# Sink scores of an attention and token-mixer kernel: from full-array matmuls to four array tiles of 64 rows by 32 columns

## The chip, the cores and the metric

The kernel runs on one core of a Trainium2 chip. A core has a matrix engine (TensorE, PE in the profile, its weight loads PEld), VectorE (DVE), ScalarE (ACT), GpSimd (POOL) and SyncE (SP), which take their instructions from five queues in order, and DMA engines. Operands lie in SBUF, matmul results in PSUM, both with 128 partitions. The metric is the time of one execution on the device in microseconds.

## The reference

Attention with a sliding window and a few sinks, followed by a mixer block, in one launch:

```python
batch, n_heads, seq, head_dim = (4, 8, 768, 64)
n_sink, window = (4, 128)
scores = scale * np.matmul(q, k.transpose(0, 1, 3, 2))
keep = is_sink | in_window          # key < 4, or 0 <= query - key < 128
a = softmax(np.where(keep, scores, -1e9))
x = a @ v                           # heads side by side: (4, 768, 512)
h = np.maximum(x.T @ w_tok1, 0) @ w_tok2      # over tokens, 768 -> 256 -> 768
u = x + h.T
out = u + np.maximum(u @ w_ch1, 0) @ w_ch2    # over channels, 512 -> 1536 -> 512
```

A query needs its own block of 128 keys, the block before, and the first four keys (the sinks). For queries of the first two blocks the sinks lie in those blocks; for the other four blocks, 512 queries a head, the scores of the four sinks are a product of their own. That product is what the change is about.

## The kernel before, in words

The 32 heads are handled as 16 pairs (`pairs`, four to a batch), the 768 tokens as six tiles of 128. q and k of a pair are turned so that the 64 elements of a head's vectors lie on partitions, head 0 of the pair on 0 to 63, head 1 on 64 to 127 (tiles qT2 and kT). The stages of a pair:

- `transposed` (line 452; `turn`, line 432, for the first five pairs) turns q and k through TensorE, with one matmul on rows 0 to 63 of the array and one on rows 64 to 127 in turn, into two PSUM banks. `prepare` lists the copies out of PSUM, among them `sink_columns`, which copies the four sink columns of each head into `kTs`.
- `scores(p, g)` (line 486): the window scores of key blocks 2g and 2g+1, again with matmuls on half of the rows, one head each, `ps[:, i]` being another bank for each head i. Exp on ScalarE (line 509), a mask on VectorE or, early on, added by TensorE (`masked`).
- `score_sinks(p)` (line 530): the sink scores of pairs p-1 and p, two matmuls over all 128 rows and 128 columns that add up in one bank (`ps_sk`), then one Exp on ScalarE into `pT_sink` (line 542). It runs once for two pairs, eight times in all.
- `sink_values` and `values` (or `pv` in the first batch and for the last pair): the weighted sums, which begin with the sinks' part; a reciprocal and a product on VectorE write `x_sb` (line 615).

`kTs` holds, for each place of a pair in its batch, a block of 128 partitions by two heads by 64 columns. It is zero but for the sinks' keys: head i's rows, in its own 64 columns, at column 0 for an even pair and at column 32 (`ODD`) for an odd one. So in the full-array product, partition 64i + c of the result holds head i of the even pair for c = 0 to 3 and of the odd pair for c = 32 to 35; the other partitions are zero, and the zero rows of `v_sink` drop them later.

`mix_h`, `mix_u` and `turned_u` do the token mixing and turn its result (`uT`, two copies out of two banks); `mix_channels(b)` has the channel mixing of a batch: 12 `v1` tiles by two halves of the tokens (four matmuls of 384 columns each, copied out with a relu), then 72 output matmuls of 512 columns in groups of three.

The kernel divides PSUM into two slots of two banks with the tag sc and four single banks with the tag mx. Everything that is not scores or transposed pairs takes mx.

The order of all instructions is decided by a planner while the program is built. A `unit` is a run of TensorE work with a cost, its dependencies, the banks it needs (all free at its start) and the work on other engines that follows. A `burst` joins several `piece`s that use half the rows into one unit, with the banks of all. `Plan.run` goes through three lists: `first` (the first batch's attention, `first_attention`, line 782), `main` (the channel mixing) and `side` (attention and token mixing of the other batches, `attention_and_tokens`, line 806), each in its own order. Between main and side it takes whichever can begin sooner, with a target for how far side should be. A change between units that use half the rows and all others is charged `SWITCH` (line 214). Costs and times of the planner only decide the order; on the chip the engines wait for each other through semaphores.

On the side, a pair p has two bursts: the first with the next pair's transposes, scores of g = 0 and the sink values of the pair before; the second with the scores of g = 1 and 2 and, for two of the four pairs of a batch, `turned_u`. For an even hp the unit `score_sinks(p + 1)` stands just before that second burst. All matmuls go through the helper `mm` (line 109), so their rows in the profile carry its line.

Of the kernel before, what the change touches and what calls it, by code (L numbers as in the profile page):

```python
# [16 lines left out]
def kernel(  # L17
# [14 lines left out]
    B, H, S, D = q.shape  # L32
    P = 128
# [7 lines left out]
    NHP = H // 2  # L41
# [21 lines left out]
    def bank(tag, *shape, dtype=FP32, slot=None):  # L63

        n = given[tag].pop(0) if slot is None else slot
        return psum.tile([P, *shape], dtype, name=f"ps_{tag}", tag=f"{tag}{n}", bufs=1)
# [41 lines left out]
    def mm(*args, **kwargs):  # L108
        in_order(nc.tensor.matmul(*args, skip_group_check=True, **kwargs))  # L109
# [19 lines left out]
    done = {}  # L129
    tiles = {}  # L130
# [7 lines left out]
    def keep_warm(n, slot):  # L138
# [18 lines left out]
        out=ident, in_=ident, compare_op=ALU.not_equal, fill=1.0, base=0, pattern=[[-1, P]], channel_multiplier=1,  # L157
    ))
    in_order(nc.gpsimd.affine_select(
        out=mask_add[:, :, 0], in_=mask_add[:, :, 0], compare_op=ALU.is_ge,  # L160
# [3 lines left out]
        out=mask_add[:, :, 1], in_=mask_add[:, :, 1], compare_op=ALU.is_ge,  # L164
# [10 lines left out]
    kTs = [kTs0[:, n] for n in range(NHP)]  # L175
# [5 lines left out]
    ODD = D // 2  # L181
# [3 lines left out]
    for n in range(4):  # L185
        i, odd = n // 2, n % 2
        rows = slice(D * i + ODD * odd, D * i + ODD * odd + n_sink)
        in_order(nc.sync.dma_start(  # L188
            out=v_sink_f[rows, odd::2, i, 0:D],
# [167 lines left out]
    def unit(ns, fn, deps=(), need=None, then=(), half=False):  # L357

        op = Op({"PE": float(ns)}, fn, deps, then, size=float(ns))
        for f in then:  # L360
            if op not in f.deps:
                f.deps.append(op)
        op.need = need or {}
        op.half = half
        return op

    def burst(*pieces):

        need = {}
        for p in pieces:  # L370
            for tag, banks in p.need.items():
                need.setdefault(tag, []).extend(banks)

        def run():
            for p in pieces:
                p.fn()

        op = unit(
            sum(p.size for p in pieces), run, [d for p in pieces for d in p.deps], need,
            [t for p in pieces for t in p.then], half=True,  # L380
        )
        for p in pieces:
            for key in p.keys:
                done[key] = op
        return op

    def piece(ns, fn, deps, need, then, keys=()):
        op = Op({}, fn, deps, then, size=float(ns))
        op.need, op.keys = need, keys
        return op  # L390
# [41 lines left out]
    def turn(p, n):  # L432

        name = ("q", "k")[n]

        def run():
            ps = [bank("mx", NT, D, dtype=BF16) for _ in range(2)]
            tiles["ps_" + name, p] = [t.rearrange("d j p -> d p j") for t in ps]
            for j in range(NT):
                for x in range(2):  # L440
                    rows = ds(D * x, D)
                    in_order(nc.tensor.transpose(ps[x][:, j], bfs[p, n][rows, j], ident[rows, rows]))

        readers = [[op] for op in done[name + "T", p]]
        if n:
            readers[0].append(done["kTs", p])
        done["t" + name, p] = unit(
            180, run, [done[name + "_bf", p]], {"mx": readers}, [op for r in readers for op in r], half=True,
        )
        return done["t" + name, p]  # L450
# [20 lines left out]
    def masked(p, g):  # L471

        def run():
            ps = tiles["ps_s", p, g] = bank("sc", 2, 4 * P)
            for i in range(2):
                mm(
                    ps[:, i, 0:width(g)], ident,
                    mask_adds[g == 0].rearrange("p k n q -> p (k n q)")[:, 0:width(g)], start=True, stop=False,
                )

        x = done["exp", p, g] = Op({}, None)
        deps = [done["tk", 0]] if p == 0 else []
        done["mask", p, g] = unit(width(g) * 0.84, run, deps, {"sc": [[x]]})
        return done["mask", p, g]
# [43 lines left out]
        return piece(width(g) * 0.47, run, deps, {} if by_pe else {"sc": [[x]]}, then, [("s", p)])  # L528

    def score_sinks(p):  # L530
        def run():
            pT_sink = pt_pool.tile([P, (NT - 2) * P], BF16, name="pT_sink")
            tiles["ps_sk", p] = bank("mx", (NT - 2) * P)
            for n in (p - 1, p):
                tiles["pT_sink", n] = pT_sink
                mm(
                    tiles["ps_sk", p], kTs[n % NHP].rearrange("p i c -> p (i c)"), tiles["qT", n][:, 2 * P:],
                    start=(n < p), stop=(n == p),
                )

        def exp(e):
            in_order(nc.scalar.activation(tiles["pT_sink", p], tiles["ps_sk", p], AF.Exp, scale=scale))

        x = Op({"ACT": 580.0}, exp, [done["pv", p - 2]] if p >= 2 else [])
        u = unit(432, run, [d for m in (p - 1, p) for d in [done["kTs", m], *done["qT", m]]], {"mx": [[x]]}, [x])
        for n in (p - 1, p):
            done["p", n, NT] = x
            done["sk", n] = u
        return u

    def pv(p, half):
        b, hp = pairs[p]
# [229 lines left out]
    def first_attention():  # L782

        for p in range(NHP):
            prepare(p)
        turned = [turn(p, n) for p in range(NHP) for n in range(2)]
        masks, scored, out = [], [], []
        for p in range(NHP):
            for g in range(NT // 2):
                if (p, g) in MASKED_BY_PE:  # L790
                    masks.append(masked(p, g))
                scored.append(burst(scores(p, g)))
                if g == 0 and p == NHP - 1:
                    scored.append(score_sinks(p))
            if p == 1:
                out.append(score_sinks(p))
            if p % 2:
                out += [pv(n, half) for n in (p - 1, p) for half in range(2)]
        tokens = []
        for g in range(2):  # L800
            tokens.append([mix_h(0, g, t, 1) for t in range(NTOK)])
            tokens[g] += [mix_u(0, g, st, 2, g == 0 or st == 2) for st in range(0, NT, 2)]
            tokens[g] += [transpose_u(0, g, st, 2) for st in range(0, NT, 2)]
        return scored, masks, turned, out, *tokens[::-1]

    def attention_and_tokens():

        parts, units = [], []
        first, last = NHP, len(pairs) - 1
        prepare(first)  # L810
        units += [turn(first, n) for n in range(2)]
        for p in range(first, last + 1):
            b, hp = pairs[p]
            pieces = []
            if p < last:
                prepare(p + 1)
                pieces.append(transposed(p + 1))
            pieces.append(scores(p, 0))
            if p > first:
                pieces.append(sink_values(p - 1))  # L820
            if p == last:
                pieces.append(turned_u(b, 0, "sc"))
            units.append(burst(*pieces))
            if p > first:
                units += [values(p - 1, i) for i in range(2)]
            pieces = [scores(p, 1), scores(p, 2)]
            if hp == 0 and p > first:
                units.append(mix_h(b - 1, 1, 0, NTOK))
                units += [mix_u(b - 1, 1, st, 2) for st in range(0, NT, 2)]
                pieces.append(turned_u(b - 1, 1))  # L830
            if hp == NHP - 1 and p < last:
                pieces.append(turned_u(b, 0))
            if hp % 2 == 0:
                units.append(score_sinks(p + 1))
            units.append(burst(*pieces))
            units[-1].then.append(sink_rows(p))
            if hp == 2:
                units.append(mix_h(b, 0, 0, NTOK))
                units += [mix_u(b, 0, st, 2) for st in range(0, NT, 2)]
            if hp == 0 and p > first:  # L840
                parts.append(units)
                units = []
        units += [pv(p, half) for half in range(2)]
        units.append(mix_h(b, 1, 0, NTOK))
        units += [mix_u(b, 1, st, 2) for st in range(0, NT, 2)]
        units.append(burst(turned_u(b, 1)))
        return parts + [units]
# [162 lines left out]
    plan.pending.append(done["masks"])  # L1010

    first = first_attention()
    main, side, sizes = [], [], []
    parts = attention_and_tokens()
    for b in range(B):
        units = parts[b] if b + 1 < B else []
# [53 lines left out]
```

## Time and profile before

| what | value |
|---|---|
| time, median of 3 runs (lowest to highest) | 209.58 us (209.21 to 210.65) |
| the profiled execution, its own time | 209.46 us |
| its span, first to last instruction | 207.7 us |
| mean granted TensorE clock | 0.998 |
| busy in 0 to 20 us: PE, VectorE, ScalarE, GpSimd | 15.94, 13.46, 15.54, 14.86 us |
| busy in 55 to 80 us: the same | 24.63, 17.37, 12.01, 22.10 us |
| busy in 120 to 150 us: the same | 29.61, 18.32, 17.93, 0.00 us |
| Exp of the sinks, x8, mean | 0.60 us |
| uT copy of 128x768 on VectorE / on ScalarE | 0.56 / 0.82 us |

A row of the timeline gives the start and the length of a run of equal instructions, both in us, the engine, the line in the kernel, the operation, what is written and read, `rows*columns` of the array for a matmul, the shape, and how many; in brackets the idle time of the engine ahead of it and what ended it. Lengths of matmuls overlap, since the next one enters the array while the last is still on its way through; distances between starts tell what the stream costs. A few matmul records are missing from the trace, weight loads are all there. The chain of waits is the path that ended last, followed back from the last instruction.

### The profile page before, as it was taken

The numbers are of one execution on the slowest core, as the hardware profiler recorded it, in microseconds if no ns is written. First come the engines' busy times: TensorE is split into PE (matmuls) and PEld (weight loads), VectorE is DVE, ScalarE is ACT, GpSimd is POOL, SyncE is SP. The second block draws the span as 40 slices with busy tenths as digits, with TensorE's granted clock in tenths as the row PEclk, the third lists the DMA queues.
The fourth block names the chain that finished last, engine by engine and source line by source line (L and its number), as shares of the span: only waits on it lengthen the run. The fifth ranks groups of instructions, "written<-read, shape, count | busy, mean of one in ns | idle before, by whom it ended". The sixth has DMA issues, their size and how long they took to land.

```text
span 207.7 us, 5034 instructions
## 1 busy us (share of the span) xinstructions
PE 198.0 (95%) x2126; PEld 119.3 (57%) x2145; DVE 114.3 (55%) x252; ACT 114.4 (55%) x202; POOL 67.5 (32%) x86
## 2 busy tenths in 40 slices
PE   6699999999999999999999999999999999999994
PEld 2345975566665665557656645666666445665443
DVE  4786664777577675867576552767674421000222
ACT  4799668878727435867684241868751103774000
POOL 6399759794699980720000000000000000000000
PEclk9999999999999999999999999999999999999999
DMA  6999999999999999795000212100001122000222
GB/s 198 283 260 182 172 174 191 156 164 201 156 159 176 185 206 195 52 70 37 3 0 5 101 51 104 51 5 0 3 0 49 56 101 101 3 0 0 101 104 101
DMA packets 73222, 21.57 MB, mean 104 GB/s; under 512 B 63216, under 2 KB 70256, under 8 KB 73200
## 3 DMA queue, kind: packets, MB, share of 16 engines
q0 software_dynamic: 67232, 11.80, 71.9%
q1 hardware_dynamic: 5968, 9.45, 12.9%
q8 instruction: 17, 0.28, 0.6%
q14 instruction: 5, 0.04, 0.1%
HBM read 26.75 MB, written 6.29 MB: 159 GB/s over the span
## 4 chain that ended last, share of the span: by engine, by line
PE 83%; DMA 6%; DVE 4%; ACT 2%; issue 2%; POOL 1%; SPq 0%; POOLq 0%; DVEq 0%
PE ps_mx L109 75%; PE ps_sc L109 5%; DMA w_tok<-in_moe_w_tok_dram 4%; DMA v_sink_f<-in_v_dram 2%; PE ps_sc L460 2%; DVE x_sb L615 1%; ACT qT L116 1%; DVE kT L118 1%; POOL v_aug L102 1%; PE ps_mx L745 1%; ACT v1T L122 1%; DVE recip L612 1%; PE ps_mx L112 1%; POOL v_sink L118 0%; SPq L188 0%
## 5 line engine op out<-in xcount | busy, mean ns | idle before, releaser
L109 PE MATMUL ps_mx<-uT,w_ch 128*128 128x384 bf16 x384 | 68.3, 326 | 0.9 <-DVE x_sb L615 0.9
L109 PE MATMUL ps_mx<-w_ch,v1T 128*128 128x512 bf16 (+2 forms) x299 | 64.2, 362 | 0.9 <-issue 0.3
L122 ACT ACTIVATE v1T<-ps_mx 128x384 bf16<-128x384 f32 x74 | 36.3, 493 | 33.7 <-PE ps_mx L109 22.9
L109 PEld LDWEIGHTS <-w_ch 128*128 128x128 bf16 x384 | 35.5, 98 | 25.0 <-DVE x_sb L615 2.5
L109 PEld LDWEIGHTS <-v1T 128*128 128x128 bf16 x312 | 28.9, 98 | 29.2
L509 ACT ACTIVATE pT<-ps_sc 128x1024 bf16<-128x1024 f32 (+1 forms) x48 | 44.4, 956 | 2.2 <-PE ps_sc L109 1.9
L884 DVE TENSOR_TENSOR o_sb<-ps_mx,u_sb 128x512 f32<-128x512 f32 x23 | 15.9, 691 | 44.6 <-PE ps_mx L109 44.6
L94 POOL DMA_DIRECT2D q_bf<-in_q_dram x24 | 19.7, 822 | 4.7 <-DMA w_ch<-in_moe_w_ch_dram 2.4
L109 PEld LDWEIGHTS <-w_tok 128*128 128x128 bf16 x192 | 18.3, 98 | 4.8 <-DMA w_tok<-in_moe_w_tok_dram 0.5
L94 POOL DMA_DIRECT2D k_bf<-in_k_dram x24 | 19.6, 820 | 3.1 <-DMA w_ch<-in_moe_w_ch_dram 1.7
L102 POOL DMA_DIRECT2D v_aug<-in_v_dram x16 | 16.4, 1028 | 10.9 <-PE ps_mx L109 8.0
L118 DVE COPY kT<-ps_sc 128x768 bf16<-128x768 bf16 x11 | 10.5, 958 | 17.0 <-ACT qT L116 17.0
L516 DVE TENSOR_TENSOR pT<-pT,mask_main 128x1024 bf16<-128x1024 bf16 (+1 forms) x24 | 14.5, 620 | 3.6 <-ACT pT L509 3.5
L109 PE MATMUL ps_sc<-qT,kT 64*128 64x256 bf16 x192 | 15.5, 262 | 0.3
L109 PE MATMUL ps_mx<-v_aug,pT 128*128 128x65 bf16 x352 | 15.3, 194 | 0.0
L716 DVE TENSOR_TENSOR u_sb<-ps_mx,x_sb 128x512 bf16<-128x512 f32 x20 | 12.7, 685 | 4.2 <-PE ps_mx L109 4.2
L109 PEld LDWEIGHTS <-pT 128*128 128x128 bf16 x352 | 13.5, 97 | 2.0 <-issue 0.6
L124 DVE TENSOR_SCALAR v1T<-ps_mx 128x384 bf16<-128x384 f32 x22 | 12.1, 554 | 2.7 <-PE ps_mx L109 2.0
L109 PE MATMUL ps_mx<-h1T,w_tok 128*128 128x256 bf16 x96 | 12.6, 273 | 0.0
L116 ACT ACTIVATE qT<-ps_sc 128x768 bf16<-128x768 bf16 x11 | 8.9, 810 | 6.4 <-PE ps_sc L460 6.2
L109 PE MATMUL ps_mx<-x_sb,w_tok 128*128 128x256 bf16 x96 | 12.0, 273 | 0.1
L615 DVE TENSOR_TENSOR x_sb<-ps_mx,recip 128x384 bf16<-128x384 f32 x22 | 11.4, 551 | 0.1
(72 smaller groups left out, 152.2 us busy)
## 6 DMA issues: line engine op xcount, KB each, us to landing
out_dram<-o_sb SPq DMA_DIRECT2D x23, 256.0 KB, 2.0
v_aug<-in_v_dram POOLq DMA_DIRECT2D x16, 192.0 KB, 6.5
w_ch<-in_moe_w_ch_dram POOLq DMA_DIRECT2D x8, 384.0 KB, 8.9
q_bf<-in_q_dram POOLq DMA_DIRECT2D x24, 96.0 KB, 6.6
k_bf<-in_k_dram POOLq DMA_DIRECT2D x24, 96.0 KB, 5.6
q_f<-in_q_dram SPq DMA_DIRECT2D x4, 384.0 KB, 5.6
k_f<-in_k_dram SPq DMA_DIRECT2D x4, 384.0 KB, 5.9
w_tok<-in_moe_w_tok_dram POOLq DMA_DIRECT2D x2, 384.0 KB, 8.1
```

Of the source, the lines that this page charges most:

```text
L94: in_order(nc.gpsimd.dma_start(out=out[:, h], in_=rows[:, h]))
L102: in_order(nc.gpsimd.dma_start(out=v_aug.rearrange("p i t d -> p (i t) d")[:, :, 0:D], in_=v[b].rearrange("h s d -> (h s) d")[2 * hp * S:2 ...
L109: in_order(nc.tensor.matmul(*args, skip_group_check=True, **kwargs))
L116: in_order(nc.scalar.activation(out, in_, AF.Copy))
L118: in_order({"DVE": nc.vector, "POOL": nc.gpsimd}[e].tensor_copy(out=out, in_=in_))
L122: in_order(nc.scalar.activation(out, in_, AF.Relu))
L124: in_order(nc.vector.tensor_scalar_max(out=out, in0=in_, scalar1=0.0))
L509: in_order(nc.scalar.activation(part(tiles["pT", p][:, :, ds(2 * g, 2)]), tiles["ps_s", p, g][:, :, 0:width(g)], AF.Exp, scale=scale,))
L516: in_order(nc.vector.tensor_tensor(out=pt, in0=pt, in1=m, op=ALU.mult))
L615: in_order(nc.vector.tensor_tensor(out=x_sb[b][:, :, ds((2 * hp + i) * D, D)], in0=tiles["ps_o", p, i][:, :, 0:D], in1=tiles["recip", p, i ...
L716: in_order(nc.vector.tensor_tensor(out=u_part(b, g, s0, n), in0=tiles["ps_u", b, g, s0], in1=x_sb[b][:, s0:s0 + n, c0:c0 + cn], op=ALU.add,))
L884: in_order(nc.vector.tensor_tensor(out=o_sb.rearrange("p (g c) -> p g c", g=2), in1=u_rows(b, st), in0=tiles["ps_out", b, st].rearrange("p ...
```

## The change

`score_sinks` computes each head of each of the two pairs with a matmul of its own: 64 rows (the head's half of the partitions), 32 columns (the block of `kTs` in which the pair's sinks stand), all 512 queries. The four write the four partition ranges 0 to 31, 64 to 95, 32 to 63 and 96 to 127 of the one bank, in that order, without adding up. The function gives a piece of cost 225 in place of a unit of cost 432. In the first attention it becomes a burst of its own; on the side it joins the second burst of the pair, as its last piece. Exp, `pT_sink` and its readers are unchanged.

```diff
             for n in (p - 1, p):
                 tiles["pT_sink", n] = pT_sink
-                mm(
-                    tiles["ps_sk", p], kTs[n % NHP].rearrange("p i c -> p (i c)"), tiles["qT", n][:, 2 * P:],
-                    start=(n < p), stop=(n == p),
-                )
+                for i in range(2):
+                    rows = ds(D * i, D)
+                    c = ODD * (n % 2)
+                    mm(
+                        tiles["ps_sk", p][ds(D * i + c, ODD)], kTs[n % NHP][rows, i, ds(c, ODD)],
+                        tiles["qT", n][rows, 2 * P:], start=True, stop=True,
+                    )
...
-        u = unit(432, run, [d for m in (p - 1, p) for d in [done["kTs", m], *done["qT", m]]], {"mx": [[x]]}, [x])
         for n in (p - 1, p):
             done["p", n, NT] = x
-            done["sk", n] = u
-        return u
+        deps = [d for m in (p - 1, p) for d in [done["kTs", m], *done["qT", m]]]
+        return piece(225, run, deps, {"mx": [[x]]}, [x], [("sk", p - 1), ("sk", p)])
...
                 if g == 0 and p == NHP - 1:
-                    scored.append(score_sinks(p))
+                    scored.append(burst(score_sinks(p)))
             if p == 1:
-                out.append(score_sinks(p))
+                out.append(burst(score_sinks(p)))
...
             if hp % 2 == 0:
-                units.append(score_sinks(p + 1))
+                pieces.append(score_sinks(p + 1))
             units.append(burst(*pieces))
```

## The prediction

> **What bounds the kernel now.** I read the page's busy row and chain first.
>
> ```profile
> span 207.7 us, 5034 instructions
> PE 198.0 (95%) x2126; PEld 119.3 (57%) x2145; DVE 114.3 (55%) x252; ACT 114.4 (55%) x202; POOL 67.5 (32%) x86
> PE 83%; DMA 6%; DVE 4%; ACT 2%; issue 2%; POOL 1%; SPq 0%; POOLq 0%; DVEq 0%
> ```
>
> TensorE is busy 95% of the span and is 83% of the chain. A nanosecond of its stream counts fully, unless the stream then waits for something else. So I next asked for the rows of the tile kTs.
>
> ```profile
> L109 PEld LDWEIGHTS <-kTs x16: 95/98/99, 10.7 to 140.1; 128*128 128x128 bf16 x16
> L109 PE MATMUL ps_mx<-qT,kTs x12: 378/379/390, 10.9 to 140.1; 128*128 128x512 bf16 x12
> ```
>
> There are 16 of these matmuls in eight groups of two (four records are missing; the weight loads show all 16). A record of 379 ns includes the way through the array; what the stream pays is the distance between starts, which the timeline of PE shows:
>
> ```profile
> 36.51 0.59 PE L109 MATMUL ps_mx<-qT,kTs 128*128 128x512 bf16 x2
> 36.94 0.81 PE L109 MATMUL ps_mx<-uT,w_ch 128*128 128x384 bf16 x4
> 37.68 0.56 PE L109 MATMUL ps_sc<-qT,kT 64*128 64x256 bf16 x8
> ...
> 41.89 0.38 PE L109 MATMUL ps_sc<-qT,kT 64*128 64x256 bf16 x4
> 42.11 0.29 PE L109 MATMUL ps_mx<-v_sink,pT_sink 64*128 64x65 bf16 x8
> ...
> 53.45 1.48 PE L109 MATMUL ps_mx<-x_sb,w_tok 128*128 128x256 bf16 x12
> 54.77 0.81 PE L109 MATMUL ps_mx<-uT,w_ch 128*128 128x384 bf16 x4
> ...
> 173.36 15.76 PE L109 MATMUL ps_mx<-uT,w_ch 128*128 128x384 bf16 x96
> 188.96 15.76 PE L109 MATMUL ps_mx<-w_ch,v1T 128*128 128x512 bf16 x94
> ```
>
> Four prices follow. A group of sink scores costs 36.94-36.51 = 0.43 us, 0.216 a matmul. A 384-column matmul costs (188.96-173.36)/96 = 0.1625, so four end their stream at 36.94+0.65 = 37.59, and the half-row scores begin at 37.68: a change of array form costs about 0.09 to 0.1, I take 0.095, the same on the way out. A full 256-column matmul costs (54.77-53.45)/12 = 0.11, but four half-row ones of that width take 42.11-41.89 = 0.22 instead of 0.44: two row halves run side by side.
>
> **The change, part by part.** In the order of PE's instructions in the changed program, six of the eight groups move from a place between full matmuls to the end of a half-row burst; the two of the first attention keep their place. Every group had two full matmuls and has four of 64x32, all 512 columns wide; the loads of weights go from two to four, narrower, and lie under the stream as now.
>
> *Streaming.* No row of this trace shows 32-column tiles. The low end is one matmul's 0.216, all four side by side; the middle 0.432, the row halves paired and the second pair of heads after the first; the high end 0.864, one by one. I take 0.22: the four use four disjoint pieces of rows and columns, and the nearest row, the row halves, adds nothing visible for its second tile. The Trainium skill (TensorE: Matmul & The Clock Gate, "Part 3: Packing small matmuls") says that tiles in different columns overlap too and that each further one adds about 4 ns; by it the group would take 0.228 and the sum below would end 0.05 us later. No row here shows column tiles.
>
> *Changes of form.* A group between full matmuls had none of its own. The new one adds the step from half rows to 64x32; its way out replaces that of the burst. 0.095 by the row above; the ends are 0 (still 64 rows) and 0.163 (the record's 0.379 less 0.216: a complete run-out) with 0.068 more on the way out. Each group in the stream: 0.095+0.22-0.432 = -0.117 us; six: -0.70.
>
> *The two groups of the first attention gain nothing.* The chain shows why:
>
> ```profile
> 11.33 7.89 DMA w_tok<-in_moe_w_tok_dram
> 19.22 0.05 issue
> 19.27 0.83 PE ps_mx L109 x6
> ```
>
> The one recorded matmul of the second group starts at 18.83; its weights load from 18.60, so it is the second of the two, and its stream ends at 18.83+0.216 = 19.05. Then PE waits 0.22 us for w_tok1, which GpSimd issues at 11.33 behind two loads of v; nothing of that hangs on PE. What is saved ahead of 19.27 lengthens that wait, and a loss of up to 0.22 is hidden by it.
>
> *Waits that go.* The new order lets two waits vanish:
>
> ```profile
> 51.44 0.38 PE L109 MATMUL ps_mx<-qT,kTs 128*128 128x512 bf16 x1
> 52.20 0.82 PE L109 MATMUL ps_mx<-uT,w_ch 128*128 128x384 bf16 x4 [0.39 <-DVE x_sb L615]
> ...
> 63.32 0.11 PEld L109 LDWEIGHTS <-kT 64*128 64x128 bf16 x3 [0.18 <-issue]
> ```
>
> The group that starts at 51.44 streams until 51.87 and the next matmul waits for a bank until 52.20: 0.33. Now six output matmuls (6 x 0.216 = 1.30) stand there before the burst. At 63.32 the scores wait 0.16 for the Exp that ends at 63.27; in the new order twelve output matmuls instead of nine stand ahead, 0.65 later. Together -0.49; the bound is 0, if their places only move.
>
> *A wait that comes.* The burst now asks for the sink bank beside its others. Where it also holds the transposes of u (pair 8, then 12) that is three of the four mx banks at once, and the plan lets the channel units take them first. At pair 8 all 72 output matmuls of batch 0 now stand ahead of the burst; before, 15 of them (3.24 us) came behind it. What follows now is the first v1 unit of batch 1, whose third matmul needs the second uT copy of that same burst. Its cost by rows of a burst of the same form:
>
> ```profile
> 104.84 0.56 PE L109 MATMUL ps_sc<-qT,kT 64*128 64x256 bf16 x8
> 105.24 0.51 PE L745 MATMUL ps_mx<-ident,u_sb 64*128 64x64 bf16 x24
> 105.68 1.47 PE L109 MATMUL ps_mx<-uT,w_ch 128*128 128x384 bf16 x8
> ...
> 105.79 1.02 DVE L118 COPY uT<-ps_mx 128x768 bf16<-128x768 bf16 x2 [0.28 <-PE ps_mx L745]
> ```
>
> Counted from the burst's first score: scores and transposes 0.84, of which 0.095 is the way out, so 0.745; the sink group 0.095+0.22; way out 0.095; two v1 matmuls 0.325; PE is at the third at 1.48. Both copies are on VectorE and end at 105.79+1.02-104.84 = 1.97, and PE starts some 0.05 later: a wait of 0.54. At pair 12, 30 output matmuls (6.5 us) still cover it. I bound it by 0 and 0.54.
>
> *ScalarE.* The sinks' Exp (0.60) now follows the burst's two (1.02 and 0.81). Its reader, the sink values of the next burst, stands nearest at pair 8: after the third v1 matmul at 2.02 come 0.325 for it and the next, 0.095, and 0.58 of transposes and scores (41.53 to 42.11), so it is due at 3.02. The burst's Exps begin 0.43 after its first score (76.45 to 76.88 in the trace) and take 1.73 together, the sinks' 0.60 more: 2.76. Elsewhere at least a dozen full matmuls lie between. If this cover went, some tenths would be paid once.
>
> **Sum.** -0.70-0.49+0.54 = -0.65 us on the profiled run's 209.46 (span 207.7 and 1.76 around it; the runs' median is 209.58, 0.12 above): 208.8. Its own range: with no price for the change of form, no new wait and both old ones gone, 6 x -0.212-0.49 = -1.76, 207.7; with the run-out price, 6 x 0.019+0.54 and neither old wait gone, +0.65, 210.1.
>
> **Rivals.** *Column tiles don't overlap* (the second pair of heads streams after the first): 0.432 in place of 0.22, so six groups cost +0.095 each, +0.57; the two early ones lose 0.19, inside the 0.22; with +0.05 of waits +0.62: 210.1, and with the run-out price 6 x 0.231 instead of 0.57, up to 211.0. For it: those matmuls share their rows' way in, and no row shows the like. Against: nothing in the trace.
>
> *Nothing overlaps, because four tiles write one bank.* Every half-row pair of the trace writes two different banks, so none shows two row halves in one bank. If the second must wait for the first, and each next one for the one ahead, a group costs 0.095+0.864-0.432 = +0.527: six +3.16, the early two 1.05-0.22 = +0.83, waits +0.05: +4.04, 213.5. It decides for "slower by 1%" (2.1 us) from a streaming price of about 0.62, three passes (8 x (0.62-0.337)-0.22+0.05). The Trainium skill has this as a rule (TensorEngine Tiling, "Restrictions and Gotchas"): row tiles can't use the same PSUM bank at the same time. Against: a half-row pair writes the same partitions of two banks, while the four tiles here write four different sets of partitions of one.
>
> *The order decides*: a wait at pair 8 or elsewhere twice as long, or none and more gone. Some 1 us either way, 207.7 to 210.
>
> **How the numbers follow.** All side by side 0.62, column tiles in turn 0.17, one bank 0.15, order 0.06. Predicted is the first case, 208.8. 207.7 to 211.0 holds the first two and most of the last. One per cent is about what a measurement of this kernel can tell from no change: faster than 207.4 needs more than every row offers, 0.04; slower than 211.6 is the one-bank case and a little of the others, 0.18; within, 0.78.
>
> **What would show it.** Four kTs records per group beginning within some 10 ns of one another, and the next full matmul about 0.31 us after the first; pairs 0.216 apart speak for the first rival, four steps of 0.216 for the second. A PE wait on uT of about half a microsecond near 78 us; none at 52; w_tok still ending the wait at 19.2. I am wrong if the step into 64x32 costs well over 0.16 or if long new waits show elsewhere on PE.

## The result, and the profile after

| | before | after |
|---|---|---|
| time, median of 20 runs each, taken together (lowest to highest) | 209.72 us (209.21 to 210.65) | 208.99 us (208.18 to 210.01) |
| ratio, 95% interval | | 0.9964 (0.9953 to 0.9976) |
| span of the profiled execution | 207.69 us | 207.41 us |
| first channel matmul to the end of the span | 176.91 us | 176.26 us |

The change gains 0.4%, some 0.7 us, and 208.8 was forecast. The page of the changed kernel, its busy row and its chain:

```profile
span 207.4 us, 5087 instructions
PE 200.7 (97%) x2161; PEld 119.5 (58%) x2161; DVE 114.7 (55%) x246; ACT 113.9 (55%) x208; POOL 67.2 (32%) x86
PE 91%; DVE 4%; DMA 2%; ACT 2%; issue 0%; SPq 0%
```

PE's busy time, which counts the time with at least one matmul record, rose although the kernel became faster. Of the 2.7 us, 1.8 lie in the first 20 us (17.70 against 15.94), where TensorE's full clock begins later in this profile (last section); besides, this trace has all its matmul records, where the one before lacks 19. The sinks' own records cover less time than before, 3.3 us against 3.9 with four of them missing. What counts is the distance between starts. The rows of the tile kTs (shortest, median and longest record in ns, then the first and last start) and PE's timeline around pair 8:

```profile
L109 PEld LDWEIGHTS <-kTs x32: 88/88/89, 11.5 to 141.2; 64*32 64x32 bf16 x32
L109 PE MATMUL ps_mx<-qT,kTs x32: 386/386/387, 11.5 to 141.2; 64*32 64x512 bf16 x32
```

```profile
78.90 0.56 PE L109 MATMUL ps_sc<-qT,kT 64*128 64x256 bf16 x8
79.30 0.51 PE L749 MATMUL ps_mx<-ident,u_sb 64*128 64x64 bf16 x24
79.74 0.40 PE L109 MATMUL ps_mx<-qT,kTs 64*32 64x512 bf16 x4
80.07 0.50 PE L109 MATMUL ps_mx<-uT,w_ch 128*128 128x384 bf16 x2
80.92 0.48 PE L109 MATMUL ps_mx<-uT,w_ch 128*128 128x384 bf16 x2 [0.35 <-DVE uT L118]
```

One record lasts 386 ns and the four together 0.40 us, so they lie on one another: in each of the six groups behind the first attention the starts lie 0, 3 or 4, 6 or 7 and 10 ns after the first. The next full matmul starts 0.328 to 0.329 us after the first tile. The last row shows the new wait. The third 384-column matmul (80.917) starts 0.676 after the second, which streams for 0.162, so PE waits 0.514; the bracket counts idle time from the modelled end of a record, and shows less. VectorE's timeline tells what it waits for:

```profile
79.01 0.69 DVE L888 TENSOR_TENSOR o_sb<-ps_mx,u_sb 128x512 f32<-128x512 f32 x1 [0.93 <-PE ps_mx L109]
79.84 1.02 DVE L118 COPY uT<-ps_mx 128x768 bf16<-128x768 bf16 x2
```

Both copies of uT run one behind the other on VectorE and end at 80.86; 0.06 later the third matmul starts.

A pair of profiles can't be subtracted as a whole, since the start differs from execution to execution (last section). I therefore use one stretch for all kernels: from the first channel matmul (30.78 before, 31.16 after) to the end of the span. From there on all kernels load the same weights, but for the sinks' own. In it the changed kernel is 176.26-176.91 = -0.65 us. Three entries account for it: six groups at -0.106 each (worked out in the section on the prediction) give -0.64, the waits at 52.20 and 63.32 that went give -0.50, the wait for uT gives +0.51; their sum is -0.63.

### The profile page after: what moved, and what is told of

Read it like the earlier page. It is cut to its first block, busy times and chain, and to the rows that moved or that the text cites. A ratio compares the mean times of both kernels' runs of the same rounds, so it can differ in the third digit from the quotient of the medians.

```text
span 207.4 us, 5087 instructions
## 1 busy us (share of the span) xinstructions
PE 200.7 (97%) x2161; PEld 119.5 (58%) x2161; DVE 114.7 (55%) x246; ACT 113.9 (55%) x208; POOL 67.2 (32%) x86
## 4 chain that ended last, share of the span: by engine, by line
PE 91%; DVE 4%; DMA 2%; ACT 2%; issue 0%; SPq 0%
PE ps_mx L109 77%; PE ps_sc L109 8%; PE ps_sc L460 2%; DMA k_f<-in_k_dram 2%; PE ps_mx L442 1%; DVE x_sb L619 1%; DVE kT L118 1%; PE ps_mx L749 1%; ACT qT L116 1%; PE ps_mx L112 1%; ACT pT L509 0%; DVE uT L118 0%; ACT v1T L122 0%; DVE recip L616 0%; DVE u_sb L720 0%
## 5 line engine op out<-in xcount | busy, mean ns | idle before, releaser
L109 PE MATMUL ps_mx<-w_ch,v1T 128*128 128x512 bf16 (+2 forms) x312 | 65.7, 363 | 0.0
```

## The experiments

All ran beside runs of the kernel before on the same chip. The diffs are against the changed kernel unless said otherwise, and no experiment leaves any work out. "Stretch" is the length from the first channel matmul to the end, less the 176.91 us of before; each value comes from one profile. The median of before differs from row to row, so the ratios are what to compare.

| kernel | median, before's beside it (us) | ratio, 95% interval | stretch (us) |
|---|---|---|---|
| the change | 208.99, 209.72 | 0.9964 (0.9953 to 0.9976) | -0.65 |
| e1: full matmuls, new place | 209.81, 209.88 | 0.9996 (0.9979 to 1.0013) | -0.13 |
| e2: tiles, old place | 210.18, 209.88 | 1.0012 (0.9996 to 1.0029) | -0.02 |
| e3: column tiles alone | 209.26, 209.88 | 0.9972 (0.9956 to 0.9989) | -0.63 |
| e4: sinks in a burst of their own | 209.10, 209.88 | 0.9966 (0.995 to 0.9982) | -0.81 |
| e5: full matmuls in the first attention | 209.00, 209.74 | 0.9973 (0.995 to 0.9996) | -0.56 |
| e6: transposes of u first | 209.02, 209.74 | 0.9963 (0.9947 to 0.9978) | -0.85 |
| e7: 64x64 tiles | 210.40, 209.74 | 1.0024 (1.0003 to 1.0045) | +0.46 |
| e8: sinks' Exp urgent | 209.11, 209.94 | 0.9973 (0.9954 to 0.9992) | -0.55 |
| e9: sinks first in the burst | 209.17, 209.94 | 0.9964 (0.9948 to 0.9981) | -0.68 |

The run e5 tells how far a stretch can be trusted: its instructions in the stretch are those of the changed kernel, and its stretch differs by 0.09, nearly all of it one wait of 0.08 at 34.18 that no other profile has. Smaller differences mean something only where the wait that makes them can be named.

### Is it the tiles or the new place? (e1, e2)

e1 keeps the order of the changed kernel and puts the two full matmuls back:

```diff
-                for i in range(2):
-                    rows = ds(D * i, D)
-                    c = ODD * (n % 2)
-                    mm(
...
-                    )
+                mm(
+                    tiles["ps_sk", p], kTs[n % NHP].rearrange("p i c -> p (i c)"), tiles["qT", n][:, 2 * P:],
+                    start=(n < p), stop=(n == p),
+                )
```

> The changed kernel with the two full-array matmuls of before in place of the four tiles; place, planner cost (225) and so the order of everything else stay as changed. Theory (the tiles' stream is the gain): in the trace of the changed kernel a group costs 0.092 for the step in, 0.010+0.216 for the four, 0.103 out in place of the burst's own 0.095, together 0.326 more than a burst without it; two full matmuls cost 0.432, so six groups give back 0.64: about 209.6. Rival (the gain is the moved order, the waits that went): it stays at 209.0.

e2 is the kernel before with the loop of tiles in place of its two matmuls; place, unit and cost stay as before.

> The kernel of before with the four 64x32 tiles, but as the unit it was, with its old cost and place, so the order is that of before. Theory (the place inside the burst is needed): between full matmuls a group pays both changes of form, 0.092+0.226+0.103 = 0.42 against 0.432: 209.6 to 209.7, no difference from before. Rival (the tiles gain wherever they stand, because a short group needs no full change): 6 x 0.2 less, 208.5; or the moved order doesn't matter and it is 209.0.

Pair 8 in e1, PE's timeline:

```profile
79.08 0.56 PE L109 MATMUL ps_sc<-qT,kT 64*128 64x256 bf16 x8
79.47 0.51 PE L746 MATMUL ps_mx<-ident,u_sb 64*128 64x64 bf16 x24
79.92 0.60 PE L109 MATMUL ps_mx<-qT,kTs 128*128 128x512 bf16 x2
80.36 0.49 PE L109 MATMUL ps_mx<-uT,w_ch 128*128 128x384 bf16 x2
81.10 0.48 PE L109 MATMUL ps_mx<-uT,w_ch 128*128 128x384 bf16 x2 [0.24 <-DVE uT L118]
```

The full group takes 0.442 from its first start to the next matmul, the tiles 0.329: 0.113 a group. But the wait for uT is 0.408 here (0.571 between the second and the third matmul, less 0.163) and 0.514 in the changed kernel: it is longer by 0.106, the gain of this one group. At pair 8 the time saved on the sinks turns into waiting, because the copies of uT end 1.96 after the burst's first score in both. The other five groups give 5 x 0.113 = 0.57, and the stretch differs by 0.52. The new place alone brings 0.13: it takes away waits of 0.50 and brings one of 0.41, which is 0.09 of it, and the rest is too small to place. Its time is that of before.

In e2 four of the six groups stand between full matmuls, the first of them here:

```profile
35.26 2.12 PE L109 MATMUL ps_mx<-uT,w_ch 128*128 128x384 bf16 x12
37.31 0.40 PE L109 MATMUL ps_mx<-qT,kTs 64*32 64x512 bf16 x4
37.64 0.82 PE L109 MATMUL ps_mx<-uT,w_ch 128*128 128x384 bf16 x4
38.40 0.56 PE L109 MATMUL ps_sc<-qT,kT 64*128 64x256 bf16 x8
```

The way in costs 0.093 (256 ns from the start of the last 384-column matmul, of which it streams 163), the way on 0.328: 0.42 in place of 0.432. Tiles that pay both changes of form themselves are worth next to nothing.

The other two groups, those of pairs 10 and 14, wait for a bank first and stand just ahead of half-row scores, and there the tiles do save time. One of them before and in e2:

```profile
92.61 0.39 PE L109 MATMUL ps_mx<-qT,kTs 128*128 128x512 bf16 x1 [0.24 <-DVE x_sb L615]
93.14 0.56 PE L109 MATMUL ps_sc<-qT,kT 64*128 64x256 bf16 x8
```

```profile
93.33 0.40 PE L109 MATMUL ps_mx<-qT,kTs 64*32 64x512 bf16 x4 [0.23 <-DVE x_sb L618]
93.66 0.76 PE L109 MATMUL ps_sc<-qT,kT 64*128 64x256 bf16 x8
```

The scores follow the group's first start by 0.329 in place of 0.538 (the record of the second matmul of before is missing), 0.21 less. But they take 0.76 in place of 0.56: their fifth matmul now waits 0.19, until 0.05 after the end of the pair's first Exp on ScalarE (94.03). At pair 14 the same numbers return. So in e2 the tiles bring nothing for two reasons, the changes of form at four places and a wait for ScalarE at two, and the stretch (-0.02) and the time show nothing. Neither part does it alone: inside a half-row burst the tiles take over a way out that the burst pays anyway.

### Which cut of the array overlaps? (e3, e7)

e3 leaves the rows whole and cuts only the columns, 128x32, four tiles:

```diff
-                        tiles["ps_sk", p][ds(D * i + c, ODD)], kTs[n % NHP][rows, i, ds(c, ODD)],
-                        tiles["qT", n][rows, 2 * P:], start=True, stop=True,
+                        tiles["ps_sk", p][ds(D * i + c, ODD)], kTs[n % NHP][:, i, ds(c, ODD)],
+                        tiles["qT", n][:, 2 * P:], start=True, stop=True,
```

> The changed kernel with tiles of 128 rows by 32 columns: each head of each pair over all rows (the other head's rows of the stationary block are zero), same place, same result. If tiles in different columns run side by side by themselves: four starts within some 10 ns, a group as dear as with 64x32, 209.0. If only the split of rows lets two run together and columns wait: four passes, 0.864 in place of 0.226, six groups +3.8, the early two some more, 213 to 213.6. If two columns' data fit at a time: two passes, +1.2 to 1.5, about 210.3.

```profile
54.46 0.56 PE L109 MATMUL ps_sc<-qT,kT 64*128 64x256 bf16 x8
54.95 0.40 PE L109 MATMUL ps_mx<-qT,kTs 128*32 128x512 bf16 x4
55.28 1.48 PE L109 MATMUL ps_mx<-x_sb,w_tok 128*128 128x256 bf16 x12
```

The starts lie 0, 3 or 4, 6 or 7 and 10 ns apart as with 64x32, and the next matmul follows after 0.331 to 0.333. The stretch is the same within 0.02, so the columns alone carry the gain. That all four share the same rows costs them nothing, which was what spoke for the first rival.

e7 uses 64x64 tiles: each head's two column blocks at once, so the two pairs must add up in the same place again.

```diff
-                        tiles["ps_sk", p][ds(D * i + c, ODD)], kTs[n % NHP][rows, i, ds(c, ODD)],
-                        tiles["qT", n][rows, 2 * P:], start=True, stop=True,
+                        tiles["ps_sk", p][rows], kTs[n % NHP][rows, i],
+                        tiles["qT", n][rows, 2 * P:], start=(n < p), stop=(n == p),
```

> The changed kernel with tiles of 64 rows by 64 columns: each head's tile covers both pairs' columns, and the two pairs add up in it, so two tiles run side by side and the second pair's two follow. Theory (a group costs 0.216 for every pass through the array, and the changes of form are the same): 0.216 more for each of eight groups, of which six certainly count: +1.3 to +1.7, 210.3 to 210.7, slower than before. Rival (the gain is the half rows and the place, not the four at once): 209.0.

```profile
80.46 0.56 PE L109 MATMUL ps_sc<-qT,kT 64*128 64x256 bf16 x8
80.85 0.51 PE L748 MATMUL ps_mx<-ident,u_sb 64*128 64x64 bf16 x24
81.30 0.62 PE L109 MATMUL ps_mx<-qT,kTs 64*64 64x512 bf16 x4
81.85 1.11 PE L109 MATMUL ps_mx<-uT,w_ch 128*128 128x384 bf16 x4
```

Now the starts are 0, 3, 240 and 243 ns: two pairs, one behind the other, 0.551 to the next matmul. That is 0.222 more a group. Four 384-column matmuls take 1.11 here and 0.81 undisturbed, since the wait for uT hides in that row: 0.294, shorter by 0.22 than after the change. So five of the six groups count, 5 x 0.222 = 1.11, and the stretch is longer than the changed kernel's by 0.46+0.65 = 1.11. This kernel is slower than before by 0.24%. It shows about what the change would have cost if column tiles had gone in turn, as the first rival of the prediction has it.

### Can the new wait be avoided? (e4, e6, e8, e9)

All four take the wait for uT away, and a gain of 0.3 to 0.5 us was expected of each. None of the ratios shows it, and the stretches show 0.2 at most.

e4 gives the sinks of pairs 8 and 12 a burst of their own ahead of the second burst:

```diff
-            if hp % 2 == 0:
+            if hp == 0 and p > first:
+                units.append(burst(score_sinks(p + 1)))
+            elif hp % 2 == 0:
                 pieces.append(score_sinks(p + 1))
```

> The changed kernel, but for the pairs whose second burst also turns u of the batch before (pairs 8 and 12) the sink scores are a burst of their own ahead of it, so that no burst asks for three mx banks; in the order six output matmuls stand behind pair 8's sink scores again, three of them behind its burst. Theory (asking for three banks lets the channel units run dry, and PE then waits 0.51 us for the uT copy at 80.4): that wait goes, two more changes of form come (2 x 0.095): -0.3, about 208.7. Rival (PE is merely ahead there and the wait comes back in another place): 209.0 to 209.2.

```profile
79.41 0.51 PE L749 MATMUL ps_mx<-ident,u_sb 64*128 64x64 bf16 x24
79.85 0.82 PE L109 MATMUL ps_mx<-w_ch,v1T 128*128 128x512 bf16 x3
80.61 0.35 PE L460 MATMUL ps_sc<-ident,q_bf 64*128 64x64 bf16 x12
80.79 0.34 PE L460 MATMUL ps_sc<-ident,k_bf 64*128 64x64 bf16 x12
81.22 0.39 PE L109 MATMUL ps_sc<-qT,kT 64*128 64x256 bf16 x4
```

The wait for uT is gone, but only three output matmuls stand behind the burst, and the next scores start at 81.22, 0.43 after the twelve matmuls on k began, where 0.18 is usual (61.36 to 61.54 after the change): 0.254 of waiting for the Exp that frees their bank. Two further changes of form of some 0.09 come on top. The stretch is 0.16 better than the changed kernel's; the ratio (0.9966 against 0.9964) is the same within its interval, which is too wide to show 0.16.

e6 lets the transposes of u stand first in that burst, so that the copies of uT begin earlier:

```diff
-                pieces.append(turned_u(b - 1, 1))
+                pieces.insert(0, turned_u(b - 1, 1))
```

> The changed kernel with the transposes of u first in the second burst of pairs 8 and 12 instead of between scores and sink scores. The copies of uT can start 0.4 us earlier, and one of the two now goes to ScalarE, ahead of the Exps. Theory (PE waits at 80.4 for the uT copies alone): counted from the end of the last output matmul both copies are there at 1.5 (ScalarE 0.65 to 1.47, VectorE's output sum until 0.89 and then 0.56), PE needs them at 1.58; the wait of 0.51 goes and nothing comes for it: about 208.5, and the time from the first token mixing matmul to the end falls from 187.87 to 187.4. Rival (the Exps start 1 us later and the wait comes back at the sink values, or main runs dry anyway): 209.0.

```profile
79.19 0.52 PE L749 MATMUL ps_mx<-ident,u_sb 64*128 64x64 bf16 x24
79.55 0.55 PE L109 MATMUL ps_sc<-qT,kT 64*128 64x256 bf16 x8
80.03 0.40 PE L109 MATMUL ps_mx<-qT,kTs 64*32 64x512 bf16 x4
80.35 3.07 PE L109 MATMUL ps_mx<-uT,w_ch 128*128 128x384 bf16 x16
```

No wait ahead of the third matmul, but the row of 16 is 3.07 long where 16 take 2.77 elsewhere in the trace of before (45.95): one of them, at 82.61, waits 0.294, at a place where a bank comes free only when ScalarE has copied v1T behind the Exps. The stretch is 0.20 better, the ratio (0.9963) the same within its interval.

e8 marks the sinks' Exp as urgent for the planner, e9 puts the sinks first in the burst. Both leave the burst's demand for three mx banks as it is.

```diff
         x = Op({"ACT": 580.0}, exp, [done["pv", p - 2]] if p >= 2 else [])
+        x.urgent = 2
```

> The changed kernel with one more line: the planner treats the sinks' Exp as urgent. In the order of the changed kernel three relu copies of v1 stand ahead of that Exp on ScalarE, and the next pair's burst, which reads its result, comes 28 v1 matmuls later; with the line the Exp follows the burst's two at once, 20 v1 matmuls stand there as before the change, and at pair 8 twelve output matmuls stand behind the burst again. Theory (the late Exp holds the side back, channel work runs dry and PE waits 0.51 us for uT at 80.4): that wait goes; the scores' wait of 0.16 near 63 may come back, since nine output matmuls stand ahead of it again: 0.35 to 0.5 less, 208.5 to 208.65. Rival (the relu copies that now wait behind the Exp hold PE up by as much): 209.0.

```diff
-                pieces.append(score_sinks(p + 1))
+                pieces.insert(0, score_sinks(p + 1))
```

> The changed kernel with the sink scores as the first piece of the burst, not the last: between them and the scores there is one change of form, as at the end, so a group should cost the same (entry from full matmuls 0.095, 0.226, then 0.095 to half rows). The sinks' Exp stands ahead of the burst's two on ScalarE, the order of the channel units is that of the run with the urgent Exp. Theory: the wait for uT goes here too, 208.5 to 208.65. Rival (the window scores' Exps, 0.6 later, delay the masks and the next pair's scores): 209.0 or a little more.

PE's and then ScalarE's timeline of e8:

```profile
76.77 0.51 PE L750 MATMUL ps_mx<-ident,u_sb 64*128 64x64 bf16 x24
77.21 0.40 PE L109 MATMUL ps_mx<-qT,kTs 64*32 64x512 bf16 x4
77.54 2.76 PE L109 MATMUL ps_mx<-w_ch,v1T 128*128 128x512 bf16 x12
80.14 0.81 PE L109 MATMUL ps_mx<-uT,w_ch 128*128 128x384 bf16 x4
```

```profile
77.66 0.60 ACT L547 ACTIVATE pT_sink<-ps_mx 128x512 bf16<-128x512 f32 x1 [4.72 <-PE ps_mx L109]
78.15 1.72 ACT L509 ACTIVATE pT<-ps_sc 128x1024 bf16<-128x1024 f32 x2
```

Twelve output matmuls stand behind the burst again and cover the copies of uT; the four v1 matmuls at 80.14 run without a gap. In both kernels the sinks' Exp stands ahead of the burst's two Exps; after the change it follows them. For e8 that is another order than was expected, which had the Exp right behind the two. The time is the changed kernel's nevertheless: the order of the plan shifts as a whole, and other waits return. The largest in e8:

```profile
83.33 0.50 PE L109 MATMUL ps_mx<-v_aug,pT 128*128 128x65 bf16 x11
83.90 0.81 PE L109 MATMUL ps_mx<-uT,w_ch 128*128 128x384 bf16 x4
...
83.33 0.52 DVE L124 TENSOR_SCALAR v1T<-ps_mx 128x384 bf16<-128x384 f32 x1
```

The last of the eleven matmuls starts at 83.63 and streams some 0.03; the next one starts 0.27 later, 0.05 after VectorE has copied a v1 tile out of its bank. That is a wait of 0.24. With 0.12 at 52.24, 0.16 at 63.03, 0.11 at 119.95 and 0.09 at 146.61, e8 has 0.72 of waits, against 0.63 after the change (0.514 at 80.92 and 0.114 at 84.88), besides four of 0.40 that both have: 0.09 more, where its stretch is 0.10 longer. e9 has 0.60 (the 0.24 at 84.30), 0.03 less, and its stretch is 0.03 shorter. So the wait for uT is gone in both and comes back elsewhere, nearly whole.

### What are the two groups of the first attention worth? (e5)

```diff
+                if p < NHP:
+                    mm(
+                        tiles["ps_sk", p], kTs[n % NHP].rearrange("p i c -> p (i c)"), tiles["qT", n][:, 2 * P:],
+                        start=(n < p), stop=(n == p),
+                    )
-                for i in range(2):
+                for i in range(2 * (p >= NHP)):
```

> The changed kernel with full-array matmuls in the two groups of the first attention alone; order and the other six groups as changed. Prediction's theory (the wait for w_tok1 takes what these two groups save): no difference, 209.0, and token mixing begins when w_tok1 lands. Rival (in most executions PE reaches token mixing only after w_tok1 has landed, as in five of the six profiles so far, so the early groups count like the others): 2 x 0.11 more, 209.2.

209.00 against 208.99, or 0.9973 against 0.9964 as ratios, decides nothing: both groups together could be worth 2 x 0.11 = 0.2 us, less than the interval of 1 us. In the profile of e5 the token mixing begins 0.216 after the second full matmul, at 19.32, and w_tok1 had landed at 19.15.

## Why the prediction was right

*Streaming and changes of form.* The four tiles run side by side: 0.216 and 10 ns for the last start, 0.226 where 0.22 was taken. The step from half rows into 64x32 is 0.092 (0.095 was taken), the way out 0.103 where the burst's own is 0.095. A group costs 0.092+0.329-0.095 = 0.326, so -0.106 against the -0.117 of the forecast, and six -0.64 against -0.70. The prediction puts all six groups between full matmuls; two of them, those of pairs 10 and 14, stood between a full matmul and half rows (92.61 and 93.14 above). Its sum hardly depends on that, since the burst's own step from full matmuls to half rows is paid in either place.

*One bank.* The rival with the chance of 0.15 falls on the same rows: four tiles write one bank and start within 10 ns. The Trainium skill (TensorEngine Tiling, "Restrictions and Gotchas") says that different row tiles cannot access the same PSUM bank simultaneously; here the two row halves do so, on different partitions, and the measurement decides. Whether the rule holds for the same partitions no run here shows. With the other rule of the Trainium skill that was weighed (TensorE: Matmul & The Clock Gate, "Part 3: Packing small matmuls", about 4 ns for a further tile) the trace agrees, with 3 to 4 ns.

*Waits that go.* Both went, for e1 and the changed kernel alike, and waits near the same places came back where the order was changed again (in e8 0.12 at 52.24 and 0.16 at 63.03). That they hang on the order and not on the tiles is shown by e1.

*The wait that comes.* It is there, from 80.40 to 80.92 (the forecast said near 78), once, 0.514 against 0.54; at pair 12 it is covered as forecast. But the reason that was given for it is not enough. The prediction blamed the burst's three mx banks, which the channel units take first. e8 and e9 ask for the same three banks and still have twelve output matmuls behind the burst, where there were 15 before. What they change is the place of the sinks' Exp on ScalarE. That the late Exp makes the plan spend the output matmuls ahead of the burst is read from these two orders; by which of the planner's terms, and whether the three banks take part in it, is not shown.

*ScalarE.* The late Exp ends at 80.95+0.60 = 81.55, 2.65 after the burst's first score (2.76 was forecast), and no wait of PE for it shows.

*The two early groups* are the step that isn't borne out. It rested on one profile, in which the mixing waited for w_tok1. After the change w_tok1 landed at 19.37 while the second group had begun at 19.22, and the mixing follows the group at once:

```profile
19.22 0.40 PE L109 MATMUL ps_mx<-qT,kTs 64*32 64x512 bf16 x4
19.55 0.83 PE L109 MATMUL ps_mx<-x_sb,w_tok 128*128 128x256 bf16 x6
```

Of the eleven profiled executions only three (before, e6 and e9) show the mixing beginning within 0.05 us of the landing. What these groups bring stays open, up to 0.2 us.

The terms of the sum came out near their forecast sizes, though the reason behind one of them does not hold. The forecast sum was -0.65, and the stretch shows -0.65: the groups gave 0.06 less and the wait cost 0.03 less than forecast, so that the two agree to the hundredth is luck. The medians differ by 0.73, with 0.5 to 1.0 as their interval.

## What to carry to other kernels

Small matmuls on disjoint columns are worth it where the stream has already left the full array: in a burst of half rows four tiles cost one, between full matmuls two changes of form of 0.09 to 0.10 us eat the gain, and what tiles alone saved just ahead of half rows (0.21) ended in a wait for ScalarE (e2). What is saved ahead of a wait whose end another engine sets lengthens that wait (pair 8: 0.408 becomes 0.514), so count the places at which the time saved reaches the end, five of six here. And where a planner writes the order, removing one wait moves others: of four orders without the wait for uT (0.51 us) two shortened the stretch by 0.16 and 0.20, one by 0.03, one made it 0.10 longer, and none changed the time measurably.

## What the runs showed that was not expected

TensorE's full speed begins at another time in each execution. The same four mask matmuls of 512 columns, after the change and before it:

```profile
6.03 1.89 PE L109 MATMUL ps_sc<-mask_add,ident 128*128 128x512 bf16 x4
```

```profile
6.68 1.04 PE L109 MATMUL ps_sc<-mask_add,ident 128*128 128x512 bf16 x4
```

They start 0.427 us apart in the first and 0.216 in the second. In the ten profiles that record the change of the granted clock the full one first comes between 4.96 (e7) and 10.88 us (after the change); in e7 it goes back to half from 8.37 to 11.78. The order of TensorE's work is the same up to the first group of sinks, and its first matmul starts at 1.46 in all. The Trainium skill (TensorE: Matmul & The Clock Gate, "Part 1: The HAM clock gate (the "warmup" mystery)") says that the release comes after some 3.4 us of activity and depends on where a free-running window stands at the start; a spread is seen here, though wider than one such window. TensorE also stands still in between here (2.17 us ahead of 7.36 in e7), so no run shows the spread under steady work.

The changed kernel's profile reaches the channel mixing 0.38 us later than before's, though the work ahead of it is not longer; that is why its span is only 0.27 shorter. Of the 0.38, 0.28 lie ahead of the token mixing, and the late clock does not explain them: in e8 the full clock comes at 9.67 and the token mixing begins at 19.32, in e1 at 5.70 and 19.62. What sets that start is not shown. The other 0.10 goes with the clock: from the first token mixing matmul to the first of the channel mixing it is 11.60 in the five profiles with the late clock (the change, e2, e3, e4, e8) and 11.50 to 11.52 in the other six.

The second full matmul behind half rows starts 227 ns after the first (e1), where 216 is usual between full matmuls.
